# A fused attention and gated feed-forward kernel: token chunks of 608 become chunks of 1024, the weights' operands are kept in DRAM and loaded pair by pair, and four of the seven operands of v have one tile

## Chip, cores, metric

The program runs on one core of one Trainium2 chip, as one launch. The metric is the device time in microseconds (us). Three runs of the kernel before gave 2260.76, 2260.9 and 2263.39 us, so the median is 2260.9 us.

## What is computed

There are 4 batches of 6080 tokens with 256 channels, and a feed-forward layer of 2048 units.

```python
qn = q / (norm(q, axis=1) + 1e-6);  kn = k / (norm(k, axis=1) + 1e-6)   # over the tokens
a  = softmax(kn.T @ qn / tau)          # 256 x 256 for each batch
x  = (v @ a).reshape(24320, 256)
h  = x @ w_in                          # w_in 256 x 2048
out = (h * sigmoid(1.702 * h)) @ w_out # w_out 2048 x 256
```

`w_in` and `w_out` come as 64-bit floats (read as pairs of 32-bit words) and are made into 32-bit floats on the chip.

## The kernel before, in words

**Precision.** A product of two 32-bit matrices is made of three matmuls: each operand is split into a high part (type fp32r) and a low part (the rest), and high by high, high by low and low by high are added in PSUM. ACT makes the high part (`cast`, L260), DVE the low part by a subtraction (`low`, L271); for some tiles DVE makes the high part too (`cast_v`, L263).

**The attention is folded into the weights.** For each batch the kernel makes S = k.T q over all tokens (L494 for batch 0, straight from 32-bit tiles; L500 for batches 1 to 3, from split tiles and spread over the batch ahead), its softmax `a` (`Attention.finish`), and then W = a w_in (`weights`, L617, its matmuls at L648). After that v W is h. The columns of w_in are taken in 4 groups (`NG`) of 4 blocks of 128 (`FG`), so a group holds 2 pairs of blocks (`PAIRS`), and there are 8 pairs (`NU`).

**Strassen's form.** A product of a pair of blocks of W (2 x 2 blocks of 128) with v (2 blocks of channels by 2 halves of tokens) is done with 7 block products in place of 8 (`P1` to `P7`, in Winograd's variant). So W and v are each turned into 7 operands (`NK`): four differences are made by DVE, and then all seven are split into high and low parts. `weights` puts the operands of a whole group into the tiles `wh0` to `wh3` and `wl0` to `wl3`, which stay in SBUF for the batch. `values` (L687) puts the seven operands of a chunk into `vh0`/`vl0` or `vh1`/`vl1`, in turn.

**Chunks and units.** The tokens of a batch are cut into 10 chunks of 608 (`NCH`), two halves of 304 columns (`HALF`). A *unit* (L720) is one pair on one chunk: 7 block products of 3 matmuls (L737, into the PSUM banks X, Y and Z), ACT copies of partial sums (`snap`), DVE additions, the gate (L753), the split of the gated rows into `gh` and `gl`, and 8 products with `w_out` of 3 matmuls (L803), which add up in four PSUM banks over the 8 units of a chunk. That is 45 matmuls of 304 columns in a unit and 360 in a chunk. After the eighth unit the sums are copied (L829, L260) and stored.

**The order** of every engine is found by a planner on the host (`Plan.order`, L86): each operation has a cost, a due time (`DUE`, in slots: a unit has 45) and the buffers it uses. Engines run their lists strictly in order.

**The start.** Batch 0 loads all of q and k first. The 64-bit weights are made into 32-bit ones by ACT and DVE (`to_float32`, L302): one group of w_in is ready before the first unit, the other three groups and most of w_out are converted while the first units run. To give that conversion time, the first two chunks of batch 0 go through the groups in turns (`rows[:2]`, L889), with sums of a part of the groups kept in the tiles `part0` and `part1` and added later. The weights of the later batches are made during the last chunk of the batch ahead.

Of the kernel before, what the change touches and what calls it, by code (L numbers as in the profile page):

```python
# [25 lines left out]
HALF = 304  # L26
# [162 lines left out]
def channel_attention_then_glu(  # L189
# [59 lines left out]
    win_f = dr.tile([NC2, P, DFF], F32, name="win_f")  # L249

# [131 lines left out]
    class Attention:  # L382
        def __init__(self, b):
            self.b = b
            self.direct = b == 0
# [12 lines left out]
        def load_direct(self, t0, room, slot, due):  # L398

            nt = min(room, T - t0)  # L400
            for src, tag in ((q, "wh"), (k, "wl")):
                t = sbuf(f"{tag}{slot}", [P, RT, C], F32, "raw_" + "qk"[tag == "wl"])
# [41 lines left out]
        def unit(self, u, due, after=(), S=None, pe_due=None, first_=True, last_=True):  # L444
# [6 lines left out]
            for i, nm in enumerate(("q", "k")):  # L451
# [24 lines left out]
                hl = sbuf(f"f{i + 2 * (u % 2)}", [P, UT, 2, C], F32R, nm + "s")  # L476
# [136 lines left out]

    P1, P2, P3, P5, P7, P6, P4 = range(7)
    NK = 7

    def weights(at, grp, due, wf=None, after=()):  # L617

# [20 lines left out]
        pw = []  # L639
        for i in range(NC2):  # L640
            pb = turning("w")

            def fn(i=i, pb=pb):
# [9 lines left out]
            n = g.add("PE", 6 * SLOT, fn, [at.a_h, at.a_l, *got], [at.aT_h, at.aT_l, wi_h, wi_l, pb], due + 6 + 6 * i)  # L653
            pw.append((pb, n))
        wh = sbuf(f"wh{grp}", [P, NK, 2, P], F32R, "wh")
        wl = sbuf(f"wl{grp}", [P, NK, 2, P], F32R, "wl")
        w1 = sbuf("t5", [P, GW], F32, "w1")
        sx = sbuf("vt", [P, 4, 2, P], F32, "sx")
        (p1, n1), (p2, n2) = pw
        v1 = lambda f: w1().rearrange("p (a f x) -> p f a x", a=2, f=2)[:, f]  # L660
        v2 = lambda: p2().rearrange("p (a f x) -> p f a x", a=2, f=2)
        c1 = cast(lambda: w1(), lambda: p1(), GW, [n1], [p1, w1], due + 13, psum=True)
        s3 = tt(lambda: sx()[:, 2], lambda: v1(1), lambda: v1(0), ALU.subtract, 256, [c1], [w1, sx], due + 16)
        s1 = tt(lambda: sx()[:, 1], lambda: v2()[:, 1], lambda: v1(1), ALU.add, 256, [c1, n2], [p2, w1, sx], due + 18)
# [4 lines left out]
        out.append(low(lambda: wl()[:, 0], lambda: v1(0), lambda: wh()[:, 0], 256, [ha], [w1, wh, wl], due + 19))
        hb = [  # L670
            cast(lambda f=f: wh()[:, (1, 6)[f]], lambda f=f: v2()[:, f], 256, [n2], [p2, wh], due + 19 + f, psum=True)
            for f in range(2)
        ]
        out += [
            low(
                lambda f=f: wl()[:, (1, 6)[f]], lambda f=f: v2()[:, f], lambda f=f: wh()[:, (1, 6)[f]], 256,
                [hb[f]], [p2, wh, wl], due + 21 + f,
            )
            for f in range(2)
        ]  # L680
        hs = cast(lambda: wh()[:, 2:6], lambda: sx(), 1024, [s4, s3], [sx, wh], due + 23)
        out.append(low(lambda: wl()[:, 2:6], lambda: sx(), lambda: wh()[:, 2:6], 1024, [hs], [sx, wh, wl], due + 25))
        return wh, wl, out
# [3 lines left out]
    def values(b, c, turn, due, after=()):  # L687
# [7 lines left out]
        r = load(lambda: raw()[:, :, :w], src, 512, after, [raw], due - 25)  # L695
# [274 lines left out]
```

## Time and profile before

| what | value |
|---|---|
| median of 3 runs | 2260.9 us |
| the profiled execution, its own time | 2260.41 us |
| its span, from the first to the last instruction | 2258.6 us |
| mean granted TensorE clock | 0.994 of full speed |
| PE, DVE, ACT busy share of the span | 99%, 73%, 63% |
| DMA, mean over the span | 53 GB/s |

A busy share is an average over stages. Here three stages differ: the start (to about 75 us, no unit has begun), the first chunks (to about 190 us, with the conversion of the weights beside the units), and the rest. Durations of matmuls overlap, so the time that one costs is read as a start-to-start distance, from the length of a run of equal ones in the chain of waits.

### The profile page before, as it was taken

The page shows a single profiled execution, that of the slowest core. Times are in us where ns is not written, and L with a number is a line of the kernel's source. Part 1 is how long each engine was busy: PE and PEld are TensorE (multiplying, and loading weights), DVE is VectorE, ACT ScalarE, POOL GpSimd, SP SyncE. Part 2 cuts the span into 40 slices and gives each one's busy share as a digit, 9 for nine tenths or more (in the row PEclk, how much of TensorE's full clock was granted, in tenths as well). Part 3 has the DMA queues.
Part 4 walks back from the last instruction along what each step waited for, and adds up shares of the span by engine and source line. Part 5 has one row for each costly group of instructions (what it writes and reads, how often), then busy time and mean ns, then how long its engine had stood idle before and what let it go on. Part 6 is the DMA issues. An engine that isn't in the chain of part 4 may idle for free.

```text
span 2258.6 us, 39406 instructions
## 1 busy us (share of the span) xinstructions
PE 2228.6 (99%) x15764; PEld 2203.8 (98%) x15764; DVE 1644.3 (73%) x3016; ACT 1429.8 (63%) x2962; POOL 5.4 (0%) x10
## 2 busy tenths in 40 slices
PE   9799999999999999999999999999999999999999
PEld 8689999999999999999999999999999999999999
DVE  7998778777676776777677777777777766666664
ACT  6566667666666666666666666666566655555554
POOL 0000000000000000000000000000000000000000
PEclk9799999999999999999999999999999999999999
DMA  7222112210111111110011111111001010000000
GB/s 280 90 73 82 50 60 70 81 39 33 39 53 60 60 58 44 61 56 26 32 50 61 51 51 60 60 42 56 25 32 51 23 45 23 23 23 23 23 12 23
DMA packets 56072, 118.93 MB, mean 53 GB/s; under 512 B 5712, under 2 KB 7760, under 8 KB 55888
## 3 DMA queue, kind: packets, MB, share of 16 engines
q1 hardware_dynamic: 55888, 116.41, 15.7%
q8 instruction: 123, 2.02, 0.4%
q14 instruction: 61, 0.50, 0.1%
HBM read 89.39 MB, written 27.00 MB: 52 GB/s over the span
## 4 chain that ended last, share of the span: by engine, by line
PE 94%; DVE 3%; DMA 1%; ACT 1%; issue 0%; SPq 0%; ACTq 0%
PE ps_o L803 46%; PE ps_X L737 23%; PE ps_Y L737 12%; PE ps_Z L737 6%; PE ps_s L500 5%; PE ps_w L648 2%; DVE acc_k L266 0%; DVE acc_q L266 0%; DMA v_raw<-in_vT 0%; DMA raw_k<-in_k 0%; DVE low L344 0%; DVE wl L271 0%; DVE gl L271 0%; SPq L257 0%; DVE sx L266 0%
## 5 line engine op out<-in xcount | busy, mean ns | idle before, releaser
L803 PE MATMUL ps_o<-gh,wo_h 128*128 128x304 f32 x2560 | 773.3, 302 | 2.1 <-DVE gh L263 2.1
L803 PE MATMUL ps_o<-gl,wo_h 128*128 128x304 f32 x2560 | 772.3, 302 | 1.2 <-DVE gl L271 1.1
L803 PE MATMUL ps_o<-gh,wo_l 128*128 128x304 f32 x2560 | 771.5, 301 | 0.0
L271 DVE TENSOR_TENSOR gl<-h,gh 128x608 fp32r<-128x608 f32 x640 | 505.9, 791 | 106.2 <-ACT gh L260 80.1
L260 ACT COPY s<-ps_X 128x304 f32<-128x304 f32 x640 | 263.8, 412 | 433.6 <-PE ps_X L737 333.2
L803 PEld LDWEIGHTS ps_o<-gh,wo_h 128*128 128x128 f32 x2560 | 481.3, 188 | 3.6 <-DVE gh L263 3.1
L803 PEld LDWEIGHTS ps_o<-gl,wo_h 128*128 128x128 f32 x2560 | 481.0, 188 | 2.6 <-DVE gl L271 2.5
L803 PEld LDWEIGHTS ps_o<-gh,wo_l 128*128 128x128 f32 x2560 | 481.3, 188 | 0.2
L737 PE MATMUL ps_X<-v_h,wh 128*128 128x304 f32 x1280 | 389.1, 304 | 2.6 <-ACT s L260 2.4
L737 PE MATMUL ps_X<-v_h,wl 128*128 128x304 f32 x1280 | 388.0, 303 | 1.0 <-DVE wl L271 1.0
L737 PE MATMUL ps_X<-v_l,wh 128*128 128x304 f32 x1280 | 387.4, 303 | 0.0
L753 ACT ACTIVATE h<-h 128x608 f32<-128x608 f32 (+1 forms) x640 | 363.6, 582 | 36.5 <-DVE h L266 34.9
L266 DVE TENSOR_TENSOR h<-ps_Y,s 128x304 f32<-128x304 f32 x320 | 151.4, 473 | 198.2 <-ACT s L260 195.7
L737 PEld LDWEIGHTS ps_X<-v_h,wh 128*128 128x128 f32 x1280 | 241.4, 189 | 5.6 <-ACT s L260 3.9
L737 PEld LDWEIGHTS ps_X<-v_h,wl 128*128 128x128 f32 x1280 | 241.4, 189 | 1.2 <-DVE wl L271 1.2
L737 PEld LDWEIGHTS ps_X<-v_l,wh 128*128 128x128 f32 x1280 | 241.6, 189 | 0.6
L266 DVE TENSOR_TENSOR h<-ps_Z,s 128x304 f32<-128x304 f32 x320 | 151.0, 472 | 109.5 <-ACT s L260 109.1
L260 ACT CAST gh<-h 128x608 fp32r<-128x608 f32 x320 | 224.8, 703 | 9.1 <-PE ps_o L803 2.2
L753 ACT ACTIVATE h<-ps_X 128x304 f32<-128x304 f32 x320 | 136.2, 426 | 145.3 <-PE ps_X L737 143.5
L266 DVE TENSOR_TENSOR h<-ps_Y,u 128x304 f32<-128x304 f32 x320 | 151.3, 473 | 80.6 <-PE ps_Y L737 79.4
L737 PE MATMUL ps_Y<-v_h,wh 128*128 128x304 f32 x640 | 194.7, 304 | 1.5 <-ACT wh L260 1.0
L737 PE MATMUL ps_Y<-v_h,wl 128*128 128x304 f32 x640 | 193.6, 303 | 0.6 <-DVE wl L271 0.6
(114 smaller groups left out, 2845.1 us busy)
## 6 DMA issues: line engine op xcount, KB each, us to landing
v_raw<-in_vT SPq DMA_DIRECT2D x40, 608.0 KB, 4.8
out_T<-osb SPq DMA_DIRECT2D x80, 304.0 KB, 2.4
raw_q<-in_q SPq DMA_DIRECT2D x69, 256.0 KB, 2.8
raw_k<-in_k SPq DMA_DIRECT2D x69, 256.0 KB, 3.3
wf<-win_f SPq DMA_DIRECT2D x24, 256.0 KB, 3.9
raw_q<-in_q SPq DMA_DIRECT2D x11, 512.0 KB, 7.3
raw_k<-in_k SPq DMA_DIRECT2D x11, 512.0 KB, 8.0
words<-in_w_in SPq DMA_DIRECT2D x8, 512.0 KB, 3.6
```

Of the source, the lines that this page charges most:

```text
L260: return g.add("ACT", act(n, psum), lambda: nc.scalar.copy(dst(), src()), deps, uses, due)
L266: return g.add("DVE", dve(n), lambda: nc.vector.tensor_tensor(dst(), a(), b(), op=op), deps, uses, due)
L271: lambda: nc.vector.tensor_tensor(dst(), src(), hi().bitcast(F32), op=ALU.subtract),
L500: nc.tensor.matmul(out, lhsT=rk()[:pp, j, l, ci], rhs=rq()[:pp, j, r, :], start=begin and m == 0, stop=last and m == 2, skip_group_check=True,
L648: nc.tensor.matmul(pb(), lhsT=l()[:, j, ci], rhs=r()[:, j, :], start=n == 0, stop=n == 3 * NC2 - 1,)
L737: nc.tensor.matmul(of(into), lhsT=l()[:, m, a, :], rhs=r()[:, m, :hw], start=begin and n == 0, stop=True, skip_group_check=True,)
L753: "ACT", act(n, psum), lambda: nc.scalar.activation(dst(), src(), AF.Gelu_apprx_sigmoid),
L803: nc.tensor.matmul(of(ob), lhsT=l[:, f, ds], rhs=rr()[:, n * hw : (n + 1) * hw], start=begin and i == 0 and m == 0, stop=end and i == 1 an ...
```

## The change

- `HALF` goes from 304 to 512, so a batch has 5 chunks of 1024 tokens and one of 960; a matmul of a unit has 512 columns, or 480 in the last chunk. A unit still has 45 of them.
- The operands of W are made pair by pair (`weights` gets a pair `p`; its matmuls have 256 columns), with the high and low parts of all seven operands in one tile of 128 x 1792. In the first chunk of batch 0 a unit uses that tile straight away. Each is stored once in a DRAM tensor `w_ops`, and every other unit loads its tile from there (`weights_again`), into three tiles in turn (`W0` to `W2`).
- Each operand of v has a tile of its own that holds both parts. P1, P2 and P6 have two tiles in turn; P3, P4, P5 and P7 have one, so the operand of the next chunk can be written only when the last product of this chunk has read it. Their due times are set by their first use.
- The interleaving of the first two chunks of batch 0 and the partial sums go. The conversion of a group of w_in and of two parts of w_out now stands beside two units.
- The raw tiles of q and k in batch 0, and the words of the 64-bit weights, lie in other buffers.

```diff
-HALF = 304
+HALF = 512
...
+    NK = 7
+    w_ops = dr.tile([2, NU, P, NK, 2, P], F32, name="w_ops")
...
-    def weights(at, grp, due, wf=None, after=()):
+    def weights(at, p, parts_, due, slot):
...
+        def fn():
+            for i in range(NC2):
...
                         nc.tensor.matmul(
-                            pb(), lhsT=l()[:, j, ci], rhs=r()[:, j, :], start=n == 0, stop=n == 3 * NC2 - 1,
+                            pb()[:, i * W2 : (i + 1) * W2], lhsT=l()[:, j, ci], rhs=r()[:, j, a * W2 : (a + 1) * W2],
+                            start=i == 0 and n == 0, stop=True, skip_group_check=True,
                         )
...
-        wh = sbuf(f"wh{grp}", [P, NK, 2, P], F32R, "wh")
-        wl = sbuf(f"wl{grp}", [P, NK, 2, P], F32R, "wl")
+        wt = sbuf(slot, [P, NK, 2, P], F32R, "w_op")
...
+        at.stored[p] = g.add(
+            "SP", 50 + 896 * 2.6, lambda: nc.sync.dma_start(w_ops[at.b % 2, p], wt().bitcast(F32)), ok, [wt], due + 20, lag=2200,
+        )
+        return wt, ok
+
+    def weights_again(at, p, due, slot):
+        wt = sbuf(slot, [P, NK, 2, P], F32R, "w_op")
+        return wt, [load(lambda: wt().bitcast(F32), w_ops[at.b % 2, p], 896, [at.stored[p]], [wt], due)]
...
+    TWICE = (P1, P2, P6)
+
+    def values(b, c, turn, due, use, after=()):
...
-        vh = sbuf(f"vh{turn}", [P, NK, HALF], F32R, "v_h")
-        vl = sbuf(f"vl{turn}", [P, NK, HALF], F32R, "v_l")
...
+            v = sbuf(f"v{m}{turn if m in TWICE else ''}", [P, 2, HALF], F32R, "v_op")
+            at_ = due + 48 + 24 * n if m in TWICE else use + DUE[what] - 20
...
+            slot = f"W{D % 3}"
+            if b == 0 and c == 0:
+                if a == 0 and grp > 0:
+                    parts = win_parts(grp, due - 40, wf)
+                W = weights(at, p, parts, due - 45, slot)
+            else:
+                W = weights_again(at, p, due - 90, slot)
+            unit(W, V[b, c], b, c, p)
...
-            if s < early:
-                if visit % 2 == 0 and a == 0 and visit // 2 + 1 < NG:
...
+            if b == 0 and c == 0 and a == 0 and grp + 1 < NG:
```

What the change moves is seen in the order of three engines.

**DVE in the first chunk.** Before (first fence) a group's conversion (`wf`, `tf`, `low`) is mixed with the additions and splits (`h`, `gl`) of units with 304 columns in a half. In the change (second fence) it is mixed with the operands of single pairs (`sx`, `w_op`) and wider splits.

```order
L271 TENSOR_TENSOR gl<-h_994,gh 128x608
L263 CAST gh<-h_1024 128x608
L271 TENSOR_TENSOR gl<-h_1024,gh 128x608
L266 TENSOR_TENSOR h_1084<-ps_Y,s_1076 128x304
L266 TENSOR_TENSOR tf<-tf,low 128x512
L266 TENSOR_TENSOR h_1096<-ps_Z,s_1090 128x304
L271 TENSOR_TENSOR win_l<-wf,win_h 128x512
L266 TENSOR_TENSOR h_1084<-ps_Y,u_1052 128x304
L271 TENSOR_TENSOR gl<-h_1050,gh 128x608
```

```order
L333 SCALAR_TENSOR_TENSOR tf<-words,tf 128x512
L268 TENSOR_TENSOR sx<-sx,w_747 128x128
L273 TENSOR_TENSOR w_op<-w_747,w_op 128x128
L341 TENSOR_SCALAR low<-tf 128x512
L268 TENSOR_TENSOR sx<-w_747,sx 128x128
L346 SCALAR_TENSOR_TENSOR low<-words,low 128x512
L273 TENSOR_TENSOR w_op<-w_747,w_op 128x2x128
L268 TENSOR_TENSOR tf<-tf,low 128x512
L273 TENSOR_TENSOR w_op<-sx,w_op 128x4x128
L273 TENSOR_TENSOR gl<-h_732,gh 128x1024
L273 TENSOR_TENSOR wo_l<-tf,wo_h 128x512
```

The same conversions now stand beside 8 units, where before they stood beside 16 smaller ones.

**SP's queue in batch 0, second chunk and later.** Before it holds the loads of q, k and v and the stores of the output; in the change the load of a pair's operands (`w_op<-w_ops`, 896 KB) stands there once for every unit.

```order
L257 DMA raw_q<-in_q 128x512
L257 DMA raw_k<-in_k 128x512
L257 DMA v_raw<-in_vT 128x2x608
L257 DMA raw_q<-in_q 128x512
L257 DMA raw_k<-in_k 128x512
L257 DMA raw_q<-in_q 128x512
L257 DMA raw_k<-in_k 128x512
L843 DMA out_T<-osb 128x608 x2
```

```order
L259 DMA w_op<-w_ops 128x1792
L846 DMA out_T<-osb 128x1024 x2
L259 DMA w_op<-w_ops 128x1792 x2
L259 DMA raw_q<-in_q 128x512
L259 DMA raw_k<-in_k 128x512
L259 DMA raw_q<-in_q 128x512
L259 DMA raw_k<-in_k 128x512
L259 DMA w_op<-w_ops 128x1792 x2
```

There are 184 such loads in all, and 32 stores of operands.

**PE at a change of chunks.** In the change, at the switch from the second to the third chunk, the tile of P7 (number 1456, then 2246; one buffer) is read by the last unit of the old chunk in the first row below and by the first unit of the new one in the last row of the second fence.

```order
L753 MATMUL ps_Y_2213<-v_op_1456,w_op_1943 128x512 x3
L819 MATMUL ps_o_1672<-gh_2075,wo_h_68 128x512
L819 MATMUL ps_o_1672<-gh_2075,wo_l_69 128x512
L819 MATMUL ps_o_1672<-gl_2083,wo_h_68 128x512
L753 MATMUL ps_X_2168<-v_op_1451,w_op_1943 128x512 x3
```

```order
L819 MATMUL ps_o_1702<-gl_2095,wo_h_68 128x512
L819 MATMUL ps_o_1713<-gh_2095,wo_h_68 128x512
L819 MATMUL ps_o_1713<-gh_2095,wo_l_69 128x512
L819 MATMUL ps_o_1713<-gl_2095,wo_h_68 128x512
L753 MATMUL ps_Y_2302<-v_op_2246,w_op_2063 128x512 x3
```

Between those two products stand 39 matmuls of 512 columns (the rows from the second of the first fence to the last but one of the second); in that time ACT and DVE have to write the new operand.

## Rows read from the trace of the kernel before

**Rows 1.** The page: busy time of the engines, and the shares of the chain of work that ended last.

```profile
PE 2228.6 (99%) x15764; PEld 2203.8 (98%) x15764; DVE 1644.3 (73%) x3016; ACT 1429.8 (63%) x2962; POOL 5.4 (0%) x10
...
PE 94%; DVE 3%; DMA 1%; ACT 1%; issue 0%; SPq 0%; ACTq 0%
```

**Rows 2.** Busy time by stretches (stretch in us, its length, then each engine's busy us with its count of instructions, the granted clock, the DMA share and GB/s).

```profile
75.00:196.80 121.80, 112.45 (x709) 103.81 (x708) 110.26 (x216) 76.48 (x160) 0.00 (x0) 0.96 0.20 63
80.00:160.00 80.00, 73.72 (x455) 67.64 (x456) 75.80 (x147) 52.69 (x112) 0.00 (x0) 0.95 0.29 94
196.80:2258.60 2061.80, 2057.14 (x14786) 2049.16 (x14784) 1474.89 (x2684) 1308.41 (x2726) 3.52 (x3) 1.00 0.14 46
```

**Rows 3.** The chain of work that ended last, in order of time: start in us, length in us, what, and how many.

```profile
70.04 5.15 PE ps_w L648 x12
...
635.02 2.78 PE ps_w L648 x12
...
652.45 2.77 PE ps_w L648 x12
...
685.09 1.43 PE ps_s L500 x12
...
714.52 1.42 PE ps_s L500 x12
...
2000.28 2.50 PE ps_o L803 x18
...
2050.43 2.51 PE ps_o L803 x18
...
2246.00 7.95 PE ps_o L803 x57
```

**Rows 4.** The same stretch, matmuls of one line alone: of L737 in the first row, of L803 in the second (PE busy with the count, then weight loads).

```profile
75.00:196.80 121.80, 61.66 (x336) 52.09 (x335) 0.96 0.20 63
...
75.00:196.80 121.80, 55.94 (x336) 49.36 (x337) 0.96 0.20 63
```

**Rows 5.** The timeline of DVE: start in us, length, line, operation; in brackets the idle time before it and what ended it.

```profile
36.51 0.69 DVE L266 TENSOR_TENSOR acc_q<-acc_q,sq 128x512 f32<-128x512 f32 x1
37.11 0.68 DVE L266 TENSOR_TENSOR acc_k<-acc_k,sq 128x512 f32<-128x512 f32 x1
...
47.83 0.48 DVE L266 TENSOR_TENSOR v_t<-v_raw 128x304 f32<-128x304 f32 x1 [4.48 <-DMA v_raw<-in_vT]
...
51.90 0.41 DVE L266 TENSOR_TENSOR acc_k<-acc_k 128x256 f32<-128x256 f32 x1
...
62.36 0.42 DVE L318 TENSOR_SCALAR tf<-tf 128x512 f32<-128x512 f32 x1
...
65.19 0.69 DVE L266 TENSOR_TENSOR tf<-tf,low 128x512 f32<-128x512 f32 x1
65.80 0.85 DVE L266 TENSOR_TENSOR v_t<-v_raw 128x304 f32<-128x304 f32 x2
...
70.02 0.69 DVE L271 TENSOR_TENSOR aT_l<-ps_t,aT_h 128x512 fp32r<-128x512 f32 x1
...
76.29 0.42 DVE L266 TENSOR_TENSOR sx<-sx,w 128x256 f32<-128x256 f32 x1
76.63 0.42 DVE L271 TENSOR_TENSOR wl<-ps_w,wh 128x256 fp32r<-128x256 f32 x1
...
104.43 0.47 DVE L263 CAST gh<-h 128x608 fp32r<-128x608 f32 x1
104.94 0.79 DVE L271 TENSOR_TENSOR gl<-h,gh 128x608 fp32r<-128x608 f32 x1
...
113.11 1.22 DVE L271 TENSOR_TENSOR wl<-sx,wh 128x1024 fp32r<-128x1024 f32 x1
114.24 0.42 DVE L323 TENSOR_SCALAR wf<-wf 128x512 uint32<-128x512 uint32 x1
```

**Rows 6.** Stretches with a low clock or a high rate of DMA (columns as in rows 2).

```profile
20.00:40.00 20.00, 20.00 (x95) 17.60 (x94) 19.77 (x35) 15.86 (x26) 0.00 (x0) 1.00 1.01 371
...
60.00:80.00 20.00, 8.49 (x25) 6.02 (x25) 17.86 (x40) 9.24 (x18) 0.00 (x0) 0.59 0.15 44
80.00:100.00 20.00, 19.07 (x105) 17.64 (x106) 18.58 (x36) 12.61 (x27) 0.00 (x0) 0.79 0.34 105
```

**Rows 7.** DMA issues: count, KB of each, median us from issue to landing.

```profile
v_raw<-in_vT SPq DMA_DIRECT2D x40, 608.0 KB, 4.8
out_T<-osb SPq DMA_DIRECT2D x80, 304.0 KB, 2.4
...
raw_k<-in_k SPq DMA_DIRECT2D x11, 512.0 KB, 8.0
```

**Rows 8.** Groups of instructions, shapes apart (busy us, mean ns of one), and the waits (us in total, times, longest us).

```profile
L260 ACT CAST ks<-raw_k 128x512 fp32r<-128x512 f32 x69 | 42.6, 618 | 0.0
...
ACT s L260 <- PE ps_X L737: 333.2, 317, 2.5
DVE h L266 <- ACT s L260: 304.8, 384, 2.9
```

More of the change, by code (lines that the diff above doesn't have):

```diff
@@ L400, in load_direct @@
             nt = min(room, T - t0)
-            for src, tag in ((q, "wh"), (k, "wl")):
-                t = sbuf(f"{tag}{slot}", [P, RT, C], F32, "raw_" + "qk"[tag == "wl"])
+            for src, tag in ((q, "q"), (k, "k")):
+                t = sbuf(RAW[tag][slot], [P, RT, C], F32, "raw_" + "qk"[tag == "k"])
                 cuts = range(nt + 1) if t0 == 0 else (0, nt)
@@ L609, in finish, with win_parts @@
             )
-    P1, P2, P3, P5, P7, P6, P4 = range(7)
-    NK = 7
-    def weights(at, grp, due, wf=None, after=()):
+    def win_parts(grp, due, wf=None, after=()):
         halves = []
@@ L638, in weights @@
             ))
[L639 to L643, printed above, removed]
+        return wi_h, wi_l, got
+    P1, P2, P4, P3, P5, P7, P6 = range(NK)
+    def weights(at, p, parts_, due, slot):
+        wi_h, wi_l, got = parts_
+        a = p % PAIRS
+        W2 = 2 * P
+        pb = turning("w")
+        def fn():
+            for i in range(NC2):
                 ci = slice(i * P, (i + 1) * P)
@@ L669, in weights @@
[L669 to L687, printed above, removed]
+        n = g.add("PE", 12 * 119, fn, [at.a_h, at.a_l, *got], [at.aT_h, at.aT_l, wi_h, wi_l, pb], due + 6)
+        w = sbuf("w1", [P, NC2, 2, P], F32)
+        sx = sbuf("sa", [P, 4, P], F32, "sx")
+        wt = sbuf(slot, [P, NK, 2, P], F32R, "w_op")
@@ new lines, in weights @@
+        s4 = tt(lambda: sx()[:, 0], lambda: v(1, 0), lambda: sx()[:, 3], ALU.subtract, P, [s2], [w, sx], due + 13)
+        ok = []
+        for k, z, src, deps, uses in (
+            (0, 1, lambda: w()[:, 0, 0:1], [c], [w]),
+            (1, 3, lambda: w()[:, 1], [c], [w]),
+            (3, 7, lambda: sx(), [s4, s3], [sx]),
+        ):
+            n = (z - k) * P
+            h = cast(lambda k=k, z=z: out(k, z, 0), src, n, deps, [*uses, wt], due + 9 + 2 * k)
+            ok.append(low(
+                lambda k=k, z=z: out(k, z, 1), src, lambda k=k, z=z: out(k, z, 0), n, [h], [*uses, wt], due + 12 + 2 * k,
+            ))
@@ L716, in channel_attention_then_glu, with unit @@
+        return out, ok
     marks = []
     outs = {}
-    parts = {}
-    def unit(W, V, b, c, grp, a, begin, end, final):
+    def unit(W, V, b, c, p):
         D = len(marks)
@@ L725, in unit @@
         hw = w // 2
-        wh, wl, w_ok = W
-        vh, vl, v_ok = V
+        wt, w_ok = W
+        v, v_ok = V
+        begin, end = p == 0, p == NU - 1
         X = turning("X")
@@ L813, in unit @@
             return
-        old = parts.get((b, c))
-        new = []
         for d in range(NC2):
-            if old is None:
-                os = sbuf(f"part{d}" if not final and c == 0 else f"os{d}", [P, NCH], F32, "osb")
-            else:
-                os = old[d][0]
+            os = sbuf(f"os{d}", [P, NCH], F32, "osb")
             ns = []
@@ L857, in channel_attention_then_glu @@
     for r, room in enumerate(sizes):
-        at.load_direct(t0, room, slot % NG, EARLY + 5 * t0)
+        at.load_direct(t0, room, slot % 4, EARLY + 5 * t0)
         t0 += room
@@ new lines, in channel_attention_then_glu @@
+    at.finish(-120.0)
+    keep_warm(18, [at.last], -118.0)
+    total = NCHUNK * NU
+    segs = [list(range(u, min(u + 2, nu))) for u in range(0, nu, 2)]
+    for b in range(B):
+        lo, hi = (NU + 1 if b == 0 else 2), total - 14
+        nxt, done, nparts = None, 0, None
+        for s in range(total):
+            c, p = divmod(s, NU)
+            grp, a = divmod(p, PAIRS)
+            D = len(marks)
+            due = 45.0 * D
+            slot = f"W{D % 3}"
[6 more added lines that the diff above has]
+            unit(W, V[b, c], b, c, p)
+            here = [marks[-1]]
+            if b == 0 and c == 0 and a == 0 and grp + 1 < NG:
+                n = grp + 1
+                for cc in range(NC2):
+                    words[n, cc] = win_words(n, cc, due - 20 + 10 * cc, f"os{cc}")
+                wf = [win_convert(n, cc, words[n, cc], due + 5 + 14 * cc, f"t{6 + cc}") for cc in range(NC2)]
+                for u in (2 * n, 2 * n + 1):
+                    words["o", u] = wout_words(u, due + 25 + 10 * (u % 2), f"os{u % 2}")
+                    wout_convert(u, words["o", u], due + 40 + 14 * (u % 2))
+            if p == (NU - 3 if b == 0 and c == 0 else 1):
+                nb, nc_ = divmod(b * NCHUNK + c + 1, NCHUNK)
@@ L932, in channel_attention_then_glu @@
                     nxt.finish(due + 45)
-                if c == last_chunk and grp > 0 and a == 0:
-                    W[grp - 1] = weights(nxt, grp - 1, due + 60, after=here)
-            if b > 0 and s == 0:
-                W[NG - 1] = weights(at, NG - 1, due + 60, after=here)
+                first = total - NU - 1
+                if s >= first and s - first < NU:
+                    n = s - first
+                    if n % PAIRS == 0:
+                        nparts = win_parts(n // PAIRS, due + 20, after=here)
+                    weights(nxt, n, nparts, due + 60, "wst")
         if nxt is not None:
```

149 lines of the change are left out of this document (50 added, 99 removed).

## The prediction

> **What bounds the kernel now.** First the page: PE is busy 99% of the span, and the chain that ended last runs over PE for 94% of it [rows 1]. A busy PE alone proves little, since matmuls overlap in the records, so I read what one costs from runs of equal matmuls in the chain [rows 3]. A run of 18 at 304 columns starts at 2000.28 us and the same run of the next chunk at 2050.43 us: 360 matmuls in 50.15 us, 139.3 ns each. At 512 columns, 12 take 2.77 to 2.78 us, 231.3 ns; I use 231.5 (the runs of six read 1.39). At 256 columns, 12 take 1.42 to 1.43 us, 119 ns. At the low clock 512 columns take 5.15 / 12 = 429 ns.
>
> Then the stretches [rows 2]: from 196.8 us on PE is busy 2057.1 of 2061.8 us, at full clock; DVE is busy 72%. There only matmul time counts. Between 80 and 160 us DVE is busy 75.8 of 80 us and PE 73.7: DVE is the engine that is full there, because the weights' conversion lies beside the units. So the kernel has two bounds, and the change touches both: fewer and longer matmuls in the long stage, and the same conversions beside fewer tokens in the early one.
>
> **The early stage.** I compare at equal work. Up to 196.8 us the kernel before has done 336 matmuls of L737 and 336 of L803 [rows 4]: 672 of 304 columns, 204,288 columns, which are 399 matmuls of 512.
>
> The start gets some 1 us shorter. Before, DVE waited 4.48 us for v until 47.83 us, and ended the last sum at 51.90 + 0.34 [rows 5]. The new chunk of v is 416 KB larger, 1.1 us at the 371 GB/s of [rows 6], but two 0.60 us additions now lie ahead of that wait. After it come one subtraction of 0.60 us and four steps of 0.34 us, so the sum ends at about 50.9 us. I take aT_l as written at 69.7 us, where it was 70.7 (70.02 + 0.69).
>
> From there to the last low part of the seventh pair's operands the new order gives DVE this, with the distances of [rows 5]: 12 conversions of 3.44 us (62.36 to 65.80), 41.3; 11 low parts of the weights of 0.60, 6.6; 17 additions of 0.60, 10.2; 10 `gl` of 1024 of 1.13 (113.11 to 114.24), 11.3; 5 `gh` casts, 3.8; 7 pairs, 13.9; 2 parts of v, 1.2. That is 88.3 us. A `gh` cast of 608 takes 0.51 (104.43 to 104.94); for 1024 I take 0.75, between 0.51 and 0.86 in proportion. A pair has five steps of 128 at 0.21 (from 0.34 at 256 and 0.60 at 512), one of 256, one of 512. DVE was busy 94.75% when it was full [rows 2]: 93.2 us. PE has 246 matmuls of 512 and 72 of 256 in that stretch, 57.0 + 8.6 = 65.5 us. So DVE sets the time, and PE sits idle for more than a quarter of it. After it PE has 153 matmuls of 512 until the 399 are done (others of the next chunk among them): 35.4 us, beside some 20 us of DVE. Sum: 69.7 + 93.2 + 35.4 = 198.3 us against 196.8, so **+1.5 us**; I write +2 for PE's low clock at the first unit. Bounds: -8, if DVE waits for nothing (-5) and the start gains more, and +14, if a fifth of DVE's rows wait for ACT or PE (93.2 / 0.8 - 93.2 = 23) and half of that is made up by work that PE has in hand.
>
> **The long stage.** Products left before: 14,400 - 672 = 13,728 x 139.3 ns = 1912.3 us. After: 7200 - 399 = 6801 of 512 x 231.5 = 1574.4 us, and 1440 of 480 columns at 217.4 ns (between 304 and 512 by the line through both), 313.1 us. Difference **-24.8 us**. Each ns of the 512-column matmul is worth 8.2 us, so this price decides. Below, the line through 256 and 304 columns (119.2 and 139.3) leads to 226.4 ns; above, cost in proportion to columns would be 139.3 x 512 / 304 = 234.6. I take the row that has this shape and type.
>
> The Trainium skill has another price, in TensorE: Matmul & The Clock Gate, Back-to-back issue gap: N / 2.4 + 2.5 ns, so 129.2 ns at 304 columns and 215.8 at 512. No row here agrees: both widths cost 10 to 16 ns more. By that rule the term would be an estimated -14 us, because it gives a matmul a smaller fixed cost to save.
>
> Matmuls of `weights` for batches 1 to 3: 144 of 512 (33.3 us) become 288 of 256 (34.3 us): **+1.0**. The end: after the last matmul (2246.00 + 7.95) come a copy and a store until 2258.6 [rows 3]. The copy grows by 176 columns, 0.18 us, and the store from 304 to 480 KB, which took 2.4 us [rows 7], by 0.5 us at 371 GB/s: **+0.6**.
>
> At nothing I cost three things. *The 184 loads.* 896 KB in place of nothing: about 80 GB/s more over the long stage, beside 46 [rows 2], where 371 were reached [rows 6]. By the order a load may start when its slot's old tile was last read; from there to the first use PE has 36 matmuls (8.3 us) once, 81 (18.7 us) in the median. For landing I take 5 to 6 us (608 KB took 4.8 [rows 7]); the bound above is 8.0 x 896 / 512 = 14 us, the rate of the crowded start. At that, ten loads would be late, by 14 us together. *The single tiles of v.* Between last and first read PE has 35 to 54 matmuls, 8 to 12 us. The new operand needs an ACT cast of 0.62 [rows 8] and a DVE step of 0.60; with the longest queue waits of [rows 8], 2.5 and 2.9, that is 6.6 us. *DVE and ACT in a unit.* The unit grows from 6.27 to 10.42 us, DVE's part to 3 x 0.60 + 2 x 1.13 + 0.75 = 4.8 us, 46%: it has room. If this cover fails, PE stands still, and its wait counts in full.
>
> **Sum**, against the profiled execution's 2260.4 us (its span 2258.6 and 1.8 around it; 0.5 below the median): 2260.4 - 24.8 + 1.0 + 0.6 + 2 = **2239 us**, 1% faster.
>
> **Rivals.**
> *A, a wider matmul is cheaper still* (226.4 ns): for it, 256 and 304 columns differ by 0.42 ns a column, the cycle at 2.4 GHz, so a fixed 12.5 ns would fit both; against it, the rows at 512. Then the term is -66 and the time 2198 us. Chance 0.11.
> *B, cost goes by columns* (234.6 ns in long runs of units): for it, 512 and 304 alone differ by 92 ns for 208 columns, near proportion; against it, again the 512 rows. The term is 0, the time 2264 us, the same as now. Chance 0.09.
> *C, slower: the switch of chunks.* There are 23 switches. If the cast of a single-tile operand, which waits for PE's last read, holds up the ACT copies queued behind it, PE's next partial sums come late, and PE has both X banks full. At 2 us for each, what a long wait costs now, the time is 2239 + 46 = 2285 us; from 0.95 us a switch the change loses. For it: ACT and DVE run strictly in order, and four operands go through both in one unit. Against it: 8 to 12 us of cover. Chance 0.12.
> *D, slower: the clock stays low in the first chunk.* PE idles there for more than a quarter of the time; before, the clock was low after the idle stretch from 60 us and returned by 100 us, when PE was 95% busy [rows 6]. PE's 65.5 us would become 131, against DVE's 93: 38 us more, 2277 us. Only 55 us or more at the low clock cost anything, since until then DVE is the longer. The skill's page says the same in general (What's actually happening: activity releases the throttle); by it PE, fuller at half speed, would soon be released. Chance 0.05.
> *E, the loads are late*: at the bound, 14 us in ten places, 2253 us. Chance 0.03.
>
> **How the numbers follow.** My case has 0.60, with 2225 to 2257 us of its own: 1 ns either way at 512 columns is 8 us, the early stage -10 to +12 around its value. About 0.2%, 4.5 us, is what a measurement of this kernel can tell from no change. Faster by more: my case, A and E, 0.74. Within it: B, 0.09. Slower: C and D, 0.17. The range takes in my case, A, B and E, 0.83: 2198 to 2265 us.
>
> **What would show it.** Runs of 12 `ps_o` matmuls in the chain should last 2.78 us, a chunk of 1024 tokens 83.3 us in the last batch. From 80 to 160 us DVE should be over 90% busy and PE below 85%; the last conversion should end near 163 us, at full clock by 100 us. After 200 us PE should have no waits over 1 us at the switches and none on `w_op`. I am wrong if the 512-column distance is off 231.5 by more than 2 ns, if PE is busy less than 99% after 200 us, or if the eighth pair starts later than 175 us.

## The result, and the profile after

The kernel after takes **2209.72 us** in the median of four runs (2208.2 to 2211.22), the kernel before 2261.6 us beside it: a ratio of **0.977, 95% interval 0.9753 to 0.9787**. It is faster by 52 us, where 21 were forecast. The profiled execution took 2208.2 us, with a span of 2206.4.

The page after, busy time and the chain (answers to [rows 1]):

```profile
PE 2170.5 (98%) x10196; PEld 1825.0 (83%) x10196; DVE 1554.9 (70%) x2288; ACT 1336.9 (61%) x2126; POOL 4.9 (0%) x10
...
PE 90%; DVE 4%; DMA 3%; ACT 1%; issue 0%; SPq 0%; ACTq 0%
```

PE still bounds the kernel, with two thirds as many matmuls. The weight loads (PEld), 98% busy before, have room now.

The stretches after (columns as in [rows 2], the last two answer to [rows 6]); 192.94 us is where the work of 204,288 product columns is done, as 196.70 us was before:

```profile
75.00:192.94 117.94, 108.38 (x479) 85.85 (x479) 113.17 (x207) 79.57 (x135) 0.00 (x0) 0.96 0.51 179
80.00:160.00 80.00, 70.44 (x320) 54.72 (x320) 78.08 (x149) 51.71 (x88) 0.00 (x0) 0.98 0.51 169
192.94:2206.40 2013.46, 2005.14 (x9443) 1688.96 (x9441) 1382.76 (x1965) 1212.58 (x1914) 3.02 (x3) 1.00 0.39 138
60.00:80.00 20.00, 10.06 (x36) 8.71 (x37) 17.96 (x44) 9.25 (x20) 0.00 (x0) 0.50 0.23 86
80.00:100.00 20.00, 17.80 (x85) 13.49 (x85) 19.61 (x40) 14.28 (x25) 0.00 (x0) 1.00 0.49 146
```

From 80 to 160 us, in the first chunk, DVE is busy 78.08 of 80 us, PE 70.44. The equal work is done 3.8 us sooner than before.

The chain after (answers to [rows 3]: start, length, what, how many):

```profile
40.52 9.00 DMA v_raw<-in_vT
...
2007.19 4.76 PE ps_o L819 x21
2017.39 4.76 PE ps_o L819 x21
2028.27 4.08 PE ps_o L819 x18
...
2109.87 4.08 PE ps_o L819 x18
...
2188.64 13.02 PE ps_o L819 x60
```

This is the surprise. 21 matmuls of 512 columns in 4.76 us are **226.7 ns** each, not 231.5. The two runs of 18 are a chunk apart: 81.60 us for 360 matmuls, 226.7 ns again. The last 60 have 480 columns: 217.0 ns, where 217.4 was forecast.

DVE's timeline after (answers to [rows 5]) and the DMA issues (as [rows 7]):

```profile
49.54 0.69 DVE L268 TENSOR_TENSOR v_t<-v_raw 128x512 f32<-128x512 f32 x1 [3.92 <-DMA v_raw<-in_vT]
...
70.33 0.69 DVE L273 TENSOR_TENSOR aT_l<-ps_t,aT_h 128x512 fp32r<-128x512 f32 x1 [0.41 <-ACT aT_h L262]
...
157.69 0.69 DVE L273 TENSOR_TENSOR w_op<-sx,w_op 128x512 fp32r<-128x512 f32 x1
```

```profile
w_op<-w_ops SPq DMA_DIRECT2D x184, 896.0 KB, 4.6
w_ops<-w_op SPq DMA_DIRECT2D x32, 896.0 KB, 4.6
v_raw<-in_vT SPq DMA_DIRECT2D x20, 1024.0 KB, 7.6
```

The account, from the starts of all matmuls in the two traces:

| part | before | after | difference | forecast |
|---|---|---|---|---|
| equal early work done at | 196.70 | 192.94 | -3.8 | +1.5 (+2 written) |
| products of the long stage, with their waits | 1915.7 | 1866.1 | -49.6 | -24.8 |
| matmuls of `weights`, batches 1 to 3 | 33.3 | 34.3 | +1.0 | +1.0 |
| from the start of the last product to the end | 5.0 | 5.2 | +0.2 | +0.6 |
| sum (spans: 2258.6 to 2206.4) | | | -52.2 | -21 |

So the question was why L648's row, same type and shape, read 231.3 ns, and the products 226.7.

### The profile page after: what moved, and what is told of

The parts are those of the page before. It is cut to its first block, busy times and chain, and to the rows that moved or that the text cites. A ratio compares the mean times of both kernels' runs of the same rounds, so it can differ in the third digit from the quotient of the medians.

```text
span 2206.4 us, 27182 instructions
## 1 busy us (share of the span) xinstructions
PE 2170.5 (98%) x10196; PEld 1825.0 (83%) x10196; DVE 1554.9 (70%) x2288; ACT 1336.9 (61%) x2126; POOL 4.9 (0%) x10
## 4 chain that ended last, share of the span: by engine, by line
PE 90%; DVE 4%; DMA 3%; ACT 1%; issue 0%; SPq 0%; ACTq 0%
PE ps_o L819 45%; PE ps_X L753 23%; PE ps_Y L753 11%; PE ps_Z L753 6%; PE ps_s L503 5%; PE ps_w L657 1%; DMA w_ops<-w_op 1%; DMA wf<-win_f 1%; DMA v_raw<-in_vT 1%; DVE gl L273 0%; DVE acc_k L268 0%; DVE h L268 0%; DVE low L346 0%; DVE acc_q L268 0%; DMA raw_k<-in_k 0%
## 5 line engine op out<-in xcount | busy, mean ns | idle before, releaser
L753 PE MATMUL ps_X<-v_op,w_op 128*128 128x512 f32 (+1 forms) x2304 | 637.0, 390 | 12.1 <-ACT s L262 8.4
L819 PE MATMUL ps_o<-gh,wo_h 128*128 128x512 f32 (+1 forms) x1536 | 597.5, 389 | 0.5 <-DVE gh L265 0.5
L819 PE MATMUL ps_o<-gl,wo_h 128*128 128x512 f32 (+1 forms) x1536 | 596.1, 388 | 0.5 <-DVE gl L273 0.5
L819 PE MATMUL ps_o<-gh,wo_l 128*128 128x512 f32 (+1 forms) x1536 | 596.5, 388 | 0.0
L273 DVE TENSOR_TENSOR gl<-h,gh 128x1024 fp32r<-128x1024 f32 (+1 forms) x384 | 466.0, 1214 | 176.9 <-ACT gh L262 156.4
L753 PEld LDWEIGHTS ps_X<-v_op,w_op 128*128 128x128 f32 x2304 | 429.3, 188 | 104.6 <-ACT s L262 12.2
L262 ACT COPY s<-ps_X 128x512 f32<-128x512 f32 (+1 forms) x384 | 222.6, 580 | 314.0 <-PE ps_X L753 260.3
L769 ACT ACTIVATE h<-h 128x512 f32<-128x512 f32 (+3 forms) x384 | 318.8, 839 | 100.3 <-DVE h L268 93.0
L753 PE MATMUL ps_Y<-v_op,w_op 128*128 128x512 f32 (+1 forms) x1152 | 323.5, 389 | 0.0
L753 PEld LDWEIGHTS ps_Y<-v_op,w_op 128*128 128x128 f32 x1152 | 215.7, 189 | 44.1 <-DVE h L268 1.9
L262 ACT COPY u<-ps_X 128x512 f32<-128x512 f32 (+1 forms) x192 | 111.8, 583 | 187.7 <-PE ps_X L753 180.5
L262 ACT CAST gh<-h 128x1024 fp32r<-128x1024 f32 (+1 forms) x192 | 199.5, 1039 | 17.9 <-PE ps_o L819 13.0
```

Source lines behind the costliest of these rows:

```text
L262: return g.add("ACT", act(n, psum), lambda: nc.scalar.copy(dst(), src()), deps, uses, due)
L273: lambda: nc.vector.tensor_tensor(dst(), src(), hi().bitcast(F32), op=ALU.subtract),
L753: nc.tensor.matmul(of(into), lhsT=wt()[:, m, l, :], rhs=v[m]()[:, r, :hw], start=begin and n == 0, stop=True, skip_group_check=True,)
L769: "ACT", act(n, psum), lambda: nc.scalar.activation(dst(), src(), AF.Gelu_apprx_sigmoid),
L819: nc.tensor.matmul(of(ob), lhsT=l[:, f, ds], rhs=rr()[:, n * hw : (n + 1) * hw], start=begin and i == 0 and m == 0, stop=end and i == 1 an ...
```

## The experiments

**1. Matmuls alone, by width.** A kernel of runs of 96 equal matmuls on fixed operands.

```diff
+    for i in range(96):
+        p, l, r = triple(i, 512)
+        mm(p, lhsT=l, rhs=r, **k3(i))  # 512, three in a bank
+    for i in range(96):
+        p, l, r = six(i)
+        mm(p, lhsT=l, rhs=r, **k6(i))  # 512, six in a bank
...
```

> This kernel only runs matmuls of one type (fp32r), one width after the other, 96 of each, on a PE that nothing else disturbs, then three mixtures; it computes nothing of the reference. Theory 1 (a fixed cost): start to start is N / 2.4 GHz plus some 13 ns at every width in a pure run: 512 columns 226.7 ns, 508 225, 480 213.3, 448 200, 304 140, 256 120 ns; the 231.5 ns that the rows before showed at 512 columns belong to a neighbourhood of other widths, so the mixtures (12 of 304, then 12 of 512) show 229 to 233 at 512, whether three or six matmuls in turn go to one bank. Rival 2 (512 is special): only 512 runs at 226.7; 480, 496 and 508 pay some 4 ns more than N / 2.4 + 13 also in a pure run. Rival 3 (the bank): six matmuls in a row into one bank cost 231 ns in a pure run too, three 226.7.

The chain of this kernel (L50 and L53 are 512 columns, three and six in a bank; L56 304, L59 480, L62 508, L77 256; the two L87 rows are 12 of 512 after 304 columns):

```profile
19.99 21.76 PE o L50 x96
41.75 21.76 PE o L53 x96
63.51 13.23 PE o L56 x96
76.73 20.80 PE o L59 x96
97.53 21.86 PE o L62 x96
...
191.02 11.52 PE o L77 x96
...
214.91 2.76 PE o L87 x12
219.33 2.72 PE o L87 x12
```

226.7 ns at 512 columns, in either grouping: the grouping by six was not it. 137.8 at 304, 216.7 at 480, 227.7 at 508, 120.0 at 256. Over N / 2.4 ns that is 13.3 at 512 and 256, but 11.1 at 304 and 16.0 at 508: no constant. Only the first block of 12 at 512, which came 12 matmuls of 304 after the run of 128 columns, read 230; this suggested that the first matmuls after narrow ones cost more, a start-up.

**2. The change with 304 columns in a half.** Everything of the change but the width.

```diff
-HALF = 512
+HALF = 304
```

> The changed kernel with halves of 304 columns again; the DRAM tiles, the pair-by-pair weights and the single tiles of v stay. If the width of the matmuls alone makes the gain (theory 1): no gain is left, and the early stage loses, since the conversions now lie beside 8 units of 304 columns: DVE has some 79 us from 71 us on, so the work that the kernel before had done at 152 us is done at about 171 us; 2275 to 2290 us in all, with 139 ns for a matmul. If the DRAM tiles or the new order make part of the gain (rival): below 2255 us. If loads of 896 KB for each 6.3 us are late: above 2290 us, with PE waiting on w_op.

Measured 2300.85 us, ratio 1.0173 (1.0158 to 1.0188); the time missed the expectation upwards. The products' distance is 139.2 ns, where it was 139.4 before. The rest is early (equal work at 213.2 us) and about 33 us of waits on PE, most of them (some 28) at 573 to 675, 1175 to 1235 and 1739 to 1802 us, where the next batch's weights are made. Its waits (total, times, longest) and pieces of its chain:

```profile
ACT w_op L262 <- DMA w_ops<-w_op: 21.2, 14, 2.9
```

```profile
1165.11 9.65 DMA wf<-win_f
...
1186.15 8.81 DMA w_ops<-w_op
...
1223.29 8.31 DMA w_ops<-w_op
```

The operands that are only stored have one tile (`wst`), so the next pair waits for a store of 8 to 9 us, longer than a unit of 6.3. The store is not alone: loads of a part of w_in (`wf<-win_f`, 256 KB) take as much of this chain, 20.5% between 1150 and 1240 us against 19.0%. In the kernel after a unit is 10.2 us and PE's waits are 7.5 us in the whole long stage. For a load PE waited once, 0.3 us. So the new data flow costs time by itself, and the width has to pay for it.

**3. 508 columns in a half.** `HALF = 508`: five chunks of 1016 tokens and one of 1000.

```diff
-HALF = 512
+HALF = 508
```

> Halves of 508 columns: five chunks of 1016 tokens and one of 1000, as many units and matmuls as the change has. Theory 1 (a fixed cost of some 13 ns at every width): the same time within 5 us, 2205 to 2213 us, 508 columns at 225 to 226 ns. Rival 2 (512 is special, other widths pay some 4 ns more): 228 to 230 ns, so some 25 us more, 2230 to 2240 us.

2234.54 us, ratio 0.9883 (0.9867 to 0.99): four columns fewer in a half, and 25 us are gone. The distance at 508 columns was 229.3 to 230.3 ns, 2.6 to 3.6 more than at 512. Experiment 1 had given 227.7: the kernel adds some 2 ns of its own at 508, none at 512. (A half of 508 columns is 2032 bytes, so its second half starts 240 bytes past a multiple of 256; experiment 7 says why that may matter, but no run isolates it.)

**4. Less for DVE in the first chunks.** The six DVE steps of w_out's conversion are left out for all parts but the first two.

```diff
+        if u < 2:
+            n = to_float32(t, "t5", raw, ready, due, True)
+        else:
+            high = lambda: raw().rearrange("p f d w -> p (f d) w")[:, :, 1]
+            n = g.add(
+                "ACT", act(GW), lambda: nc.scalar.activation(t(), high().bitcast(F32), AF.Abs), [ready], [raw, t], due,
+            )
```

> Leaves out the six DVE steps of the conversion of w_out for the six parts that are converted beside the first units (the output is not the reference's). If DVE sets the time of the first chunk: 20.6 us of DVE go, PE's 65 us come close to DVE's 68, and the time falls by 15 to 20 us, to about 2190 us, with DVE still over 85% busy. If PE's own work or ACT sets it: no change, 2208 us.

2198.29 us in one run; the equal work is done at 183.0 us, 9.9 sooner, where 15 to 20 were expected. From 80 to 160 us:

```profile
80.00:160.00 80.00, 75.33 (x357) 61.68 (x358) 72.91 (x133) 57.48 (x99) 0.00 (x0) 1.00 0.55 198
```

DVE set this stretch, as the prediction said, but with a little less for it PE, at 75.33 of 80, is as full.

**5. Is it a start-up?** Runs of narrow matmuls, each followed by 48 of 512.

```diff
+    for i in range(48):
+        p, l, r = triple(i, 256)
+        mm(p, lhsT=l, rhs=r, **k3(i))  # 48 of 256
+    for i in range(48):
+        p, l, r = triple(i, 512)
+        mm(p, lhsT=l, rhs=r, **k3(i))  # 512 after 48 of 256
...
```

> Only matmuls run here (nothing of the reference is computed): runs of 12, 48 or 192 narrow ones (304, 256, 480, 128 columns), each followed by 48 of 512. Question: where do the 231 ns come from that a 512-column matmul took in L648's runs of 6 and 12 in the kernel before, when pure runs take 226.7? Theory S (start-up): after a long run of narrow matmuls the first dozen of 512 take 229 to 236 ns, 4 ns more in the mean than 226.7, and the rest 226.7; so 12 narrow ones ahead leave no trace, 48 and 192 do, and the mean of the first 12 is 230 to 232 ns and of the last 24 is 226.7. Rival P (place): the 231 come from what the kernel does beside them (DVE and ACT at work on the same memory) or from that line's tiles; then every 512-column matmul here takes 226.7 from the first on, whatever ran ahead of it.

The chain, 48 of 512 after 192 of 304 (L65) and after 192 of 256 (L83):

```profile
77.15 10.88 PE o L65 x48
...
140.06 10.91 PE o L83 x48
```

All operands here start at multiples of 256 bytes. After 304 columns there is no start-up at all (226.7). After 256, however many, five matmuls read 229 to 236 ns, 0.03 us together; after 128, ten read more. So a start-up exists, but after the 304 columns that run ahead of L648 it is not there.

**6. L648 five times over**, in the kernel before.

```diff
-                for l, r in ((at.aT_h, wi_h), (at.aT_h, wi_l), (at.aT_l, wi_h)):
+                for l, r in ((at.aT_h, wi_h), (at.aT_h, wi_l), (at.aT_l, wi_h)) * 5:
```

> The kernel before with the six matmuls of L648 for each bank issued five times over (30 in a row in a bank, 60 for a group, same operands; W comes out five times too large, so the output is not the reference's). Theory S: the first 12 of a run read 229 to 236 ns as before, and the last 30 settle at 226.7; a run of 60 lasts 13.65 to 13.70 us, and the time is 2261 + 768 x 0.2267 = 2435 us. Rival P: the line's tiles or the engines beside it set 231.3 ns for all; a run of 60 lasts 13.85 to 13.90 us.

```profile
704.58 13.98 PE ps_w L648 x60
```

2442.05 us in one run. 13.98 / 60 = 233.0 ns: the **start-up theory fell**. The first 12 of a run of 60 read 231 to 232 ns in the mean, so less than the rest and not more; from the thirteenth on the six distances repeat every six matmuls to the last one (236, 227, 236, 234, 232, 235 ns, a mean of 233.3). That points to something steady in the operands, not to the chance of what runs beside them.

**7. The operands' addresses.** In the compiled program L648's moving rows start at 128 or 0 bytes modulo 256 and its weights at 192 or 0; a row of 304 columns is 1216 bytes, 4.75 x 256, so the rows of the kernel before start anywhere in steps of 64. A row of 512 is 2048 bytes: in the kernel after every 512-column product has both operands at 0. This kernel shifts the two operands alone.

```diff
+    def triple(i, w, mo=0, wo=0):
+        m0, w0 = mo // 4 + 512 * (i % 2), wo // 4 + P * (i % 8)
+        return o[(i // 3) % 4][:, :w], st[:, w0 : w0 + P], x[:, m0 : m0 + w]
```

> Only matmuls run here (nothing of the reference is computed). The run with L648 five times over showed no settling: 60 matmuls took 13.97 us, 232.8 ns each, so theory S fell. What sets L648 apart from the products of the kernel after is where its operands lie: modulo 256 bytes its moving rows start at 128 or 0 and its weights at 192 or 0, while all operands of the 512-column products after start at 0; in the kernel before, the rows of 304 columns start at 0, 64, 128 and 192. Here runs of 36 go through 16 pairs of start bytes (moving rows at +0, +64, +128, +192, weights the same) at 512 columns, and through six pairs at 480, 304 and 256. Theory A (address): the distance depends on the start bytes; at 512 columns pairs that differ in them read 231 to 233 ns and (0, 0) reads 226.7. Rival P (the kernel beside it): the addresses do not matter, every pair reads 226.7 at 512, 216.7 at 480, 137.8 at 304, 120 at 256, and what DVE, ACT and the DMAs do beside the matmuls is left.

The chain: L45, L48, L51, L54 have the weights at +0 and the rows at +0, +64, +128, +192; L57 and L60 have the weights at +64 and the rows at +0 and +64 (512 columns); L111, L117 are 304 columns with rows at +0 and +128, L129, L138 256 columns with rows at +0 and +192; L108 (480 columns) has the rows at +0 and the weights at +128, L141 (256 columns) the rows at +0 and the weights at +64:

```profile
20.11 8.16 PE o L45 x36
28.27 8.26 PE o L48 x36
36.53 8.37 PE o L51 x36
44.90 8.40 PE o L54 x36
53.30 8.40 PE o L57 x36
61.70 8.18 PE o L60 x36
...
191.97 7.91 PE o L108 x36
199.88 4.96 PE o L111 x36
...
209.81 5.04 PE o L117 x36
...
229.86 4.32 PE o L129 x36
...
242.69 4.09 PE o L138 x36
246.78 4.24 PE o L141 x36
```

At 512 columns only the distance in bytes from the weights' start to the rows' start counts, modulo 256 (from here on "distance" alone means this one, and the time from start to start is the price). The last 24 prices of each run, in ns:

| columns | 0 | 64 | 128 | 192 |
|---|---|---|---|---|
| 512 (16 pairs, each distance four times) | 226.7 | 228.9 | 232.1 to 232.8 | 233.3 |
| 480 (weights at +0; in brackets moved, rows at +0) | 216.7 | 218.3 | 217.8 (220.0) | 216.2 (215.9) |
| 304 (the same) | 137.8 | 137.8 | 140.0 (140.0) | 138.7 (138.7) |
| 256 (the same) | 120.0 | 117.8 | 118.5 (118.6) | 113.3 (117.8) |

At 480 and 256 columns the same distance, made with the weights in place of the rows, can have another price (220.0 for 217.8, 117.8 for 113.3), so there the distance alone does not settle it.

L648 has the distances 192, 64 and 128 in equal parts: (233.3 + 228.9 + 232.1) / 3 = 231.4 ns, near its row's 231.3. That the two meet so closely is in part luck: in long runs the same operands settle at 233.3 (experiment 6), so a mixture of distances is not priced by its mean. Its price was right for its operands and wrong for those of the products.

**8. Undone inside the kernel.** The kernel after, its products' weights 64 bytes later.

```diff
+    LATER = {"W0": 64, "W1": 64, "W2": 64}
...
+        later = LATER.get(slot, 0)
...
+    sb.tile([P, 16], F32, name="pad0")
     wo_h = sb.tile([P, NF, C], F32R, name="wo_h")
     wo_l = sb.tile([P, NF, C], F32R, name="wo_l")
+    sb.tile([P, 48], F32, name="pad1")
```

> The kernel after with all weights of the products (the three tiles W, and w_out's two) 64 bytes later in SBUF; nothing else moves against them, so every 512-column product has its moving rows 192 bytes past its weights, modulo 256. Theory A (the distance between the start bytes sets the price): the isolated runs gave 233.33 ns for that distance against 226.67 for none, so 6801 products of the long stage cost 45 us more and the rest of the early stage 1 us: 2255 us, runs of 12 ps_o in 2.80 us, a full chunk in 84.0 us. 480 columns stay near 216 to 218. Rival P (what works beside PE sets the price): 2209 to 2213 us.

```profile
2054.90 4.90 PE ps_o L832 x21
2066.10 4.20 PE ps_o L832 x18
...
2229.05 13.04 PE ps_o L832 x60
```

**2248.66 us**, ratio 0.9946 (0.9929 to 0.9962), 39 us more by 64 bytes. 4.90 / 21 = 233.3 ns, the isolated price to the digit; 480 columns stay at 217. The expectation of 45 us took 226.7 as the base; the mean over the kernel after is 227.4, with its start-ups, and 6800 x 5.9 ns is 40.

**9. Equal starts for 304 columns.** Experiment 2 with each half at a multiple of 320 columns.

```diff
-            v = sbuf(f"v{m}{turn if m in TWICE else ''}", [P, 2, HALF], F32R, "v_op")
+            v = sbuf(f"v{m}{turn if m in TWICE else ''}", [P, 2, 320], F32R, "v_op")
...
-                                of(ob), lhsT=l[:, f, ds], rhs=rr()[:, n * hw : (n + 1) * hw],
+                                of(ob), lhsT=l[:, f, ds], rhs=rr()[:, n * 320 : n * 320 + hw],
```

> The kernel after with HALF = 304, as in an earlier run (2300.85 us), but with each half's 304 columns at a multiple of 320 columns, so that moving rows and weights all start at a multiple of 256 bytes; before, a half started 0, 64, 128 or 192 bytes past its weights. It says how much of 139.3 ns at 304 columns is address. Theory A: the isolated runs gave 137.8 ns at no distance and a mean of 138.6 over the distances that the kernel had, so 14,400 products cost 11 us less, and up to 21 us if the mixed order cost more than its mean: 2280 to 2290 us. Rival P: 2297 to 2304 us.

2282.02 us, 19 us less than 2300.85. The chains, 15 matmuls of `ps_o`, of experiment 2 and of this one:

```profile
2281.24 2.09 PE ps_o L819 x15
```

```profile
2263.10 2.06 PE ps_o L819 x15
```

Over the long stage the products took 137.9 ns in place of 139.2, the isolated 137.8 nearly. The gain is nearer the upper end of the expectation: the mixed order cost more than the mean of its distances (138.6).

**10. Another distance at 256 columns.** f0 (split q, w_in's high part) 192 bytes later.

```diff
+    LATER = {"f0": 192}
```

> The kernel after with one tile (f0, the split q of batches 1 to 3 and w_in's high part) 192 bytes later. In isolated runs 256 columns took 113.3 ns at that distance and 120.0 at none. Theory A: 864 matmuls of L503 and 256 of the weights' 384 take up to 6.7 ns less, 7.5 us if groups of 12 behave as long runs; the first few of a group take the old price, so 3 to 7 us: 2203 to 2207 us. Rival P: 2209 to 2211 us.

2204.03 us, ratio 0.9748 (0.9733 to 0.9763): some 5 us less, but not as expected. The 256-column matmuls of L503 went from 118.9 to 117.8 ns only. Short groups are not the reason: the isolated run read 113 to 114 ns from the fourth matmul on, and here the seventh to the twelfth still read 117.5 to 118.5. It is the price that experiment 7 read for the same distance with the weights moved (L141), so at 256 columns something besides the distance counts, and what it is stays open. Most of the gain came from what follows them. PE's timeline behind a group of 256 columns, of the kernel after, and of this one:

```profile
720.25 0.40 PE L819 MATMUL ps_o<-gh,wo_h 128*128 128x512 f32 x1
720.49 0.40 PE L819 MATMUL ps_o<-gh,wo_l 128*128 128x512 f32 x1
720.72 0.39 PE L819 MATMUL ps_o<-gl,wo_h 128*128 128x512 f32 x1
```

```profile
717.49 0.39 PE L830 MATMUL ps_o<-gh,wo_h 128*128 128x512 f32 x1
717.72 0.39 PE L830 MATMUL ps_o<-gh,wo_l 128*128 128x512 f32 x1
717.95 0.39 PE L830 MATMUL ps_o<-gl,wo_h 128*128 128x512 f32 x1
```

The three take 0.47 us from first to third start after, 0.46 here, and of the 12 matmuls behind such a group hardly any reads over 228 ns here, five did after: the start-up is gone, and the mean of all 512-column products fell from 227.4 to 226.9 ns, 2.9 us over 6800.

**11. One tile for every operand of v, and 12. two tiles for W.**

```diff
-    TWICE = (P1, P2, P6)
+    TWICE = ()
```

> The kernel after with one tile for each of the seven operands of v (no operand has two). It puts a price on the switch of chunks, the rival called C in the prediction. If the 9.5 us between the last and the first read of an operand (42 matmuls of 226.7 ns) cover the cast and the low part, as they seem to for the four single ones, the time is 2209 to 2214 us and PE shows no wait over 1 us at a switch. If three more single tiles crowd ACT and DVE at a switch, each of 23 switches costs 0.5 to 2 us: 2221 to 2255 us.

```diff
-            slot = f"W{D % 3}"
+            slot = f"W{D % 2}"
```

> The kernel after with two tiles in turn for the operands of W in place of three, so that a load of 896 KB may start only when the unit before last has ended its products: cover falls to less than one unit (about 45 matmuls, 10.2 us, less what the products of the next unit leave), against a landing of 4.6 us. Theory (loads have room to spare): 2209 to 2213 us. Rival E (late loads): PE waits on w_op in many units; at 1 us in half of 184 units 2300 us, and the waits name the DMA.

2205.27 us (2203.9 to 2206.22) and 2209.44 us (2206.97 to 2209.93). Neither the single tiles (rival C) nor the loads (rival E) cost time, even with all operands single, and with two tiles for W, where PE waited for a load once, 0.3 us. With all single it is a little faster: the first product starts at 74.4 us in place of 76.7. Why was not isolated; experiment 13 has the same single tiles and starts at 76.3.

**13. Put together.** Experiments 10 and 11, the high part of the second gated tile by ACT in the first chunk, and two tiles for the operands that are only stored.

```diff
+    LATER = {"f0": 192}
...
-    TWICE = (P1, P2, P6)
+    TWICE = ()
...
-        r2 = split(h2, [g2], f"2{D % 2}", cast_v)
+        r2 = split(h2, [g2], f"2{D % 2}", cast if D < NU else cast_v)
...
-                    weights(nxt, n, nparts, due + 60, "wst")
+                    weights(nxt, n, nparts, due + 60, f"wst{n % 2}")
```

> The kernel after with four edits: one tile for each operand of v (2205.3 us alone), f0 192 bytes later, the high part of the second gated tile made by ACT instead of DVE during the first chunk (DVE sets that stretch; 7 casts of 0.75 us, of which half came back when six additions were left out), and two tiles in turn for the operands that are only stored. If the gains add: 2205.3 - 5 - 3 - 1 = 2196 us, 2192 to 2202. If ACT becomes late in the first chunk, or the gain of single tiles and that of the cast are the same time counted twice: 2200 to 2205.

**2195.62 us**, ratio 0.9715 (0.97 to 0.9729): faster than both kernels. The sum came out as expected, its parts did not. The equal work is done at 190.6 us (190.9 with single tiles alone), so the cast by ACT gave almost nothing. The largest part that can be told lies with the two store tiles: the wait of the kernel after, `ACT w_op L262 <- DMA w_ops<-w_op: 13.6, 8, 2.8`, is gone, and the 480-column products, beside which the next weights are made, took 312.0 us, where they took 317.9 in the kernel after and 315.6 with the single tiles alone. No run has the two store tiles alone.

## Why the prediction was wrong, step by step

- **The failed step: the price of a 512-column matmul.** The prediction took L648's row, "the row that has this shape and type". Type and shape do not fix the price: the distance between the two operands' start bytes does as well (experiments 7 and 8): L648's operands lie 64, 128 and 192 bytes apart modulo 256, those of the products 0. The price came out at 226.7 in runs and 227.4 in the mean; 6802 x 4.1 ns is 28 us, against a forecast that was 24.8 us short here (the waits below took some back). The prediction said that this price decides, and its own sign of being wrong, a time off 231.5 ns by more than 2, came true. 2209.72 us is outside the 2225 to 2257 of its own case; the wider range holds it only through rival A.
- **What the 49.6 us consist of.** At the 137.9 ns of experiment 9 the 13,728 products before would have taken 1892.8 us in place of 1913.5: 20.7 us are the end of unequal starts. From there to the products after without their waits, 1858.7, are 34.1 us of width: fewer matmuls, each with 11 to 16 ns besides its columns. Waits on PE rose from 2.3 to 7.5 us, 5.2 given back, most at the store tile (experiment 13). The first number carries 304 columns of another kernel over to this one.
- **480 columns** at 217.4 ns: right (217.1 in the mean), but by luck, since the upper end of its line was off.
- **Rival A** had the price, 226.4, and the time, 2198 us, nearest of all, but by luck. Its reason, a fixed 12.5 ns, is not borne out: with equal starts 304 columns have 11.1 ns and 480 have 16.7 over N / 2.4.
- The Trainium skill (TensorE: Matmul & The Clock Gate, Back-to-back issue gap) gives N / 2.4 + 2.5 ns, which it calls the gap of an isolated matmul, so an estimated -14 us. The trace disagrees: 226.7 ns and not 215.8 at 512 columns, and -49.6 us.
- **The early stage**: +1.5 forecast, -3.8 measured. aT_l was written at 71.0 us (69.7 forecast; v landed later, after 9.0 us). The last step of the seventh pair's operands ended at 158.4 us (162.9 forecast), so the stretch took 87.4 us, not 93.2. The row of that stretch (columns as in [rows 2]):

```profile
71.02:158.38 87.36, 77.12 (x343) 60.71 (x343) 84.23 (x168) 54.63 (x95) 0.00 (x0) 0.93 0.48 160
```

DVE was busy 84.2 us, where the prediction summed the same steps to 88.3, so the sum was 4.1 us too high; and it idled 3.1 us, where 4.9 were laid on. The rest, 34.6 us for some 153 matmuls, is again 226 ns. PE was busy 88% from 80 to 160 us, where less than 85% was forecast.

- **Weights** +1.0 and **tail** +0.6: +1.0 and +0.2. **At nothing**: loads landed in 4.6 us in the median (5 to 6 estimated), with no wait of PE on them; experiments 11 and 12 show the cover was ample.
- **Rivals B, C, D, E** did not occur. For D: clock 0.50 from 60 to 80 us, but 1.00 from 80 to 100, though PE was only 89% busy.

## What to carry to other kernels

Read a matmul's price from a row whose operands also start at the same distance modulo 256 bytes, or price both, for at 512 columns a row of the same shape was off by 2 to 3% here. When a tile is cut into halves, try columns that make a multiple of 256 bytes, or pad the rows to one: in this case 64 bytes were worth 39 us of 2209 at 512 columns, and padding 19 us at 304. At 256 and 480 columns measure it, since there the distance did not settle the price.

## What was not expected of the hardware

- The time from start to start of fp32r matmuls depends on the start of the moving rows relative to the weights, modulo 256 bytes: 226.7 to 233.3 ns at 512 columns, in the isolated runs and in the kernel (experiments 7 and 8). The best distance tried differs by width: 0 at 512, 192 at 256 (113.3 against 120.0 ns), but at 256 only with the rows moved in the isolated run: with the weights moved it read 117.8, and in the kernel, with the rows moved, 117.8 as well (experiment 10). Why is open; the isolated runs tried only multiples of 64 bytes.
- With equal starts, the part over N / 2.4 ns is 13.3 ns at 512, 384, 320 and 256 columns, but 16 at 508, 496, 480 and 448 and 11 at 304 (experiment 1).
- After narrow matmuls the first 512-column ones can cost more: five read 229 to 236 ns after 256 columns, none after 304 or 480 (experiment 5). With f0 192 bytes later that goes (experiment 10).
